# A dense last stage planned step by step: one list scheduler for every engine, and half of its output weights loaded early

## The chip, the cores and the metric

The kernel runs on one core of one Trainium2 chip. The core has five engines with a queue of instructions each: TensorE (PE, matrix products, with its weight loads shown as PEld), VectorE (DVE), ScalarE (ACT), GpSimd (POOL) and SyncE (SP), which issues most DMA transfers. An engine takes its instructions in the order in which they were written; it waits for the others through semaphores. The metric is the device time of one execution in microseconds (us). Before the change three runs took 922.58, 923.99 and 924.15 us.

## The reference

```python
# attention through 32 memory slots, 4 x 576 tokens (2304 in all), 8 heads of 64
a = softmax(phi, axis=sequence);  k_m, v_m = a.T @ k, a.T @ v
x = softmax(q @ k_m.T / 8) @ v_m                    # x: 2304 x 512
# mixture of experts: each token goes to 2 of 8 experts (512 -> 1024 -> 512)
out[token] = sum over its 2 experts of weight * (relu(x @ w1[e]) @ w2[e])
# dense last stage (512 -> 2048 -> 512)
h = out @ w_in
result = (h * cos(h)) @ w_out
```

All inputs are float32. The kernel carries each factor of a product as a high and a low float16 part and sums three products (high x high, low x high, high x low).

## The kernel before

The 2304 tokens are 18 tiles of 128. Attention and routing come first, then the eight experts (each over 5 tiles of gathered tokens), then the last stage. An expert's first layer (`l1`, tile `h`) is one group of 12 products per 128 of the 1024 columns, drained by ACT and DVE into `hT` (`l1_out`); its second (`l2`, tile `y`) makes 24 products per token tile, drained by ACT and written by DMA to a table `yd` in DRAM (`l2_out`).

The last stage goes by chunks of tiles: (0,2), (2,4), (4,8), (8,12), (12,16), (16,18). Here the chunks of two tiles are called narrow, those of four wide, and the first is chunk 0. What is done per tile `t` is `comb` (L962): POOL issues two gathers of rows of `yd` into `y0`, `y1`; ACT scales `y0` (L974); DVE adds the scaled `y1` (L975), finds the row's largest magnitude (L978), and makes a power-of-two scale and its inverses in six operations on one column each (L153 to L158, L981, L982); ACT and DVE split the row into a high and a low part `chl` (L984, L985); SP issues a transposing DMA into `x2T`. `c_bct` (L989) spreads the inverse scales of a chunk over all partitions by PE transposes `pb`, and ACT copies them to `bct`.

What is done per chunk and per 128 of the 2048 inner columns is called a unit here; each chunk has 16, f = 0 to 15. `m1` (L1027) makes 12 products `g` of 256 or 512 columns into one PSUM bank. Then come four DVE operations and two of ACT: `ty` (L1044, from PSUM), `tt` (L1045, rounding), `tt` (L1046, the remainder), ACT's sine (L1047), `ty` (L1048, from PSUM again, after which the bank is free), ACT's high part (L1049). POOL subtracts for the low part (L1050). `m2_` (L1052) multiplies both parts into output banks `o`, three products of 512 columns per tile, and after f = 15 ACT scales the bank out (L1066) and issues the store.

What sets the order: `at(t, fn)` records a call with a planned time and `issue` writes the calls in the order of these times. `chain(key, fn)` pins an operation behind the last one of the same key; what is not chained may be moved by the framework's own scheduler. In the last stage only the PE products are chained. PE's order is written out by a loop:

```python
    LAG = 3
...
        if u >= LAG:
            j, f = units[u - LAG]
            at(x, m2_, j, f)
```

so that `m2_` of a unit stands three units behind its `m1`. The times of `comb` and `c_bct` come from a formula on the start of the chunk before. `m1` takes its banks in turn from three (`ke` twice, `ha`), `m2_` from four. Row buffers: `l` (7 of 2 KB per partition) holds `y0`, `y1`, `chl` and the outputs; `s` (5 of 8 KB) holds raw expert weights earlier and `gT` in the last stage, four units to a buffer; `w` (4 of 16 KB) holds expert weights, then `win` and `wout`. Both halves of `wout` take such a `w` buffer, which comes free when the last expert's layers are done.

## Time and profile before

| | |
|---|---|
| time, median of 3 runs | 923.99 us |
| profiled execution, its own time | 923.57 us |
| its span in the trace | 921.8 us (1.77 us lie outside) |
| first product of the last stage | 532.54 us |
| first product of 512 columns there (chunk 2) | 619.91 us |
| last group of products begins | 910.03 us |
| PE busy, by engine record | 879.5 us (95%) |
| DVE / ACT / POOL busy | 583.5 / 467.7 / 215.0 us |

Products overlap on PE, and their ends are modelled, so "busy" says only that none was missing. How far apart two groups start is what PE really takes: 12 products of 256 columns about 1.31 us, six of 512 about 1.30 us. A wait shows as idle time before a row, with the engine and operation that ended it. For DVE, ACT and POOL a row's length is that of the operation and includes what it was held up after its start.

### The profile page before, as it was taken

How to read it: one execution, taken by the hardware profiler on the slowest of the kernel's cores; microseconds unless marked ns; L12 is line 12 of the kernel's file. 1: busy time of each engine (PE TensorE's matmuls, PEld its weight loads, DVE VectorE, ACT ScalarE, POOL GpSimd, SP SyncE). 2: the span in 40 equal slices, each digit the busy share in tenths (PEclk: the TensorE clock that was granted, in tenths of full speed). 3: DMA queues.
4: the chain of work that ended last, by engine and by line, in shares of the span. 5: the costliest groups of instructions: out<-in, count | busy, mean ns of one | idle time of the engine just before them, and what ended most of it. 6: DMA issues, size and time to landing. Idle time of an engine off the chain costs nothing.

```text
span 921.8 us, 14177 instructions
## 1 busy us (share of the span) xinstructions
PE 879.5 (95%) x5368; PEld 511.1 (55%) x5368; DVE 583.5 (63%) x1266; ACT 467.7 (51%) x830; POOL 215.0 (23%) x234
## 2 busy tenths in 40 slices
...
GB/s 352 395 298 90 116 159 254 268 278 240 235 256 252 289 236 282 231 307 266 206 197 113 171 160 67 95 46 69 80 1 13 155 17 12 68 12 1 1 46 23
DMA packets 108246, 146.55 MB, mean 159 GB/s; under 512 B 65808, under 2 KB 66448, under 8 KB 106128
## 3 DMA queue, kind: packets, MB, share of 16 engines
...
## 4 chain that ended last, share of the span: by engine, by line
PE 79%; DVE 7%; DMA 4%; issue 4%; ACT 3%; POOL 2%; SPq 0%; POOLq 0%; ACTq 0%; DVEq 0%
PE y L219 22%; PE h L219 21%; PE g L219 15%; PE o L219 15%; DMA y<-yd,sidx 2%; PE x L689 2%; PE kp L589 1%; DVE tt L1046 1%; PE sc L659 1%; DMA kvt<-in_kv 1%; DVE ty L1044 1%; ACT tt L1047 1%; DVE tt L1045 1%; POOL gT L1050 1%; POOL y L968 1%
## 5 line engine op out<-in xcount | busy, mean ns | idle before, releaser
L219 PE MATMUL h<-x,w 128*128 128x384 f16 (+1 forms) x1536 | 215.4, 302 | 9.7 <-DMA x<-xg 8.4
L219 PE MATMUL y<-w,hT 128*128 128x512 f16 x960 | 210.5, 379 | 0.0
L219 PE MATMUL g<-x2T,win 128*128 128x256 f16 (+1 forms) x1152 | 203.7, 327 | 4.5 <-DVE ty L1048 3.8
L219 PE MATMUL o<-wout,gT 128*128 128x512 f16 x864 | 202.6, 380 | 0.3 <-POOL gT L1050 0.2
L219 PEld LDWEIGHTS <-w 128*128 128x128 f16 x1536 | 151.6, 99 | 68.8 <-DMA x<-xg 8.5
L219 PEld LDWEIGHTS <-win 128*128 128x128 f16 x1152 | 113.2, 98 | 88.7 <-issue 5.7
L219 PEld LDWEIGHTS <-hT 128*128 128x128 f16 x960 | 93.9, 99 | 109.0
L1050 POOL TENSOR_TENSOR gT<-ty,gT 128x256 f16<-128x256 f32 (+1 forms) x96 | 93.0, 970 | 252.0 <-ACT gT L1049 249.8
L1047 ACT ACTIVATE tt<-tt,hp 128x256 f32<-128x256 f32 (+1 forms) x96 | 58.9, 614 | 163.2 <-DVE tt L1046 149.0
L219 PEld LDWEIGHTS <-gT 128*128 128x128 f16 x864 | 84.4, 98 | 93.9 <-POOL gT L1050 1.9
L219 DVE SCALAR_TENSOR_TENSOR w<-raw,wsc,w 128x1024 f16<-128x1024 f32 x64 | 81.1, 1287 | 32.8 <-ACT w L219 32.7
L219 DVE SCALAR_TENSOR_TENSOR hT<-h,hT 128x384 f16<-128x384 f32 (+1 forms) x128 | 61.5, 487 | 61.1 <-ACT hT L219 61.0
L1044 DVE SCALAR_TENSOR_TENSOR ty<-g,wis,bct 128x256 f32<-128x256 f32 (+1 forms) x96 | 58.8, 613 | 64.3 <-PE g L219 62.3
L1048 DVE SCALAR_TENSOR_TENSOR ty<-g,fac,tt 128x256 f32<-128x256 f32 (+1 forms) x96 | 59.1, 616 | 52.9 <-ACT tt L1047 52.4
L219 ACT ACTIVATE hT<-h 128x384 f16<-128x384 f32 (+1 forms) x128 | 55.3, 435 | 73.5 <-PE h L219 69.1
L1049 ACT ACTIVATE gT<-ty 128x256 f16<-128x256 f32 (+1 forms) x96 | 50.2, 523 | 64.5 <-DVE ty L1048 64.4
L829 POOL DMA_INDIRECT xg<-xd,idxB x24 | 26.0, 1085 | 216.0 <-DMA x<-xg 204.0
L219 ACT ACTIVATE w<-raw,wsc 128x1024 f16<-128x1024 f32 x64 | 71.7, 1140 | 5.0 <-ACT o L219 2.2
L1046 DVE SCALAR_TENSOR_TENSOR tt<-tt,ty 128x256 f32<-128x256 f32 (+1 forms) x96 | 68.5, 713 | 2.6
L219 ACT ACTIVATE junk<-raw 128x1024 bf16<-128x1024 f32 x64 | 67.3, 1052 | 3.8 <-ACT o L219 3.3
L219 ACT ACTIVATE o<-y,ysc 128x512 f32<-128x512 f32 x40 | 27.5, 686 | 68.2 <-PE y L219 68.2
L968 POOL DMA_INDIRECT y<-yd,sidx x36 | 36.1, 1002 | 87.4 <-DMA yd<-o 79.7
...
## 6 DMA issues: line engine op xcount, KB each, us to landing
...
yd<-o ACTq DMA_DIRECT2D x40, 256.0 KB, 6.7
...
xd<-hl SPq DMA_DIRECT2D x18, 256.0 KB, 2.4
```

The lines of the kernel that those rows point to most:

```text
L219: last[key] = fn(*a, **kw)
L589: T.matmul(kp[32 * j:32 * j + 32, g, :], lhsT=es[i][:, 32 * h:32 * h + 32], rhs=kvv[:, :, h * D:(h + 1) * D], start=(i == 0), stop=(i == 4))
L659: T.matmul(sc[p0:p0 + n, 64 * c:64 * c + 64], lhsT=qt[t // 8][:, c, c0:c0 + n], rhs=bdkt[b][:, c, :], start=True, stop=True)
L689: last[f"t{t}P"] = T.matmul(x[pn, g, 0:272], lhsT=eT[:, g, pn], rhs=bdv[b][:, g, :], start=True, stop=True)
L829: G.indirect_dma_start(out=g, out_offset=None, in_=xd[0:NA * P] if part == 0 else xd, in_offset=bass.IndirectOffsetOnAxis(ap=idx[:, col:co ...
L968: G.indirect_dma_start(out=y, out_offset=None, in_=yd[0:rows], in_offset=bass.IndirectOffsetOnAxis(ap=sidx[:, t, k:k + 1], axis=0))
L1044: V.scalar_tensor_tensor(y, ph[:, :n], wis[:, 2 * E + c:2 * E + c + 1], bct[j], op0=OP.mult, op1=OP.mult)
L1046: V.scalar_tensor_tensor(t, t, MAGIC, y, op0=OP.subtract, op1=OP.subtract)
L1047: A.activation(t, t, AF.Sin, bias=hp, scale=-2.0 * math.pi)
L1048: V.scalar_tensor_tensor(y, ph[:, :n], fac[:, c:c + 1], t, op0=OP.mult, op1=OP.mult)
L1049: A.activation(g[:, 0, :n], y, AF.Copy)
L1050: G.tensor_tensor(g[:, 1, :n], y, g[:, 0, :n], op=OP.subtract)
```

## The change

All of the last stage becomes one list of steps. `op` notes a step's engine, its assumed cost, what it calls and which steps it needs; `settle` places the whole list. Its inner `place` takes the steps by rank and puts each into the earliest free gap of its engine after its inputs; that is done forward, backward from the end and forward again, six times, and the best forward placement gives the planned times. Each step is now chained on its engine, the DMA issues of SP too, so the engines' order is the planner's and no longer the framework's.

With it: `comb` is cut into nine steps and the four operations between `m1` and `m2_` into seven; `LAG` is 4; `m1` of chunk 0 turns over five banks and that of the other chunks over three; `chl` takes buffers of the experts' gathered rows, and the outputs a buffer per chunk. The second half of `wout` goes, as two loads of 1 MB, into two of the five `s` buffers at a time within the last expert (`X[7]` is its start), which leaves three for `gT`; the first half stays in a `w` buffer and is issued 15.4 us before the planned start of the stage. The last two tiles' outputs leave by SP, and the last one is scaled half by ACT and half by DVE.

```diff
+    plan = []
+    LAT = dict(P=0.20, A=0.20, V=0.15, G=0.20, S=0.05, D=0.0)
+    ROUNDS = 6
+    def op(eng, cost, fn, *deps, lat=None):
+        flat = []
+        for d in deps:
+            flat += d if isinstance(d, (list, tuple)) else [d]
+        plan.append((eng, cost, fn, [d for d in flat if d is not None], LAT.get(eng, 0.0) if lat is None else lat))
+        return len(plan) - 1
+    def settle(goal, origin):
...
+        tail = [0.0] * n
+        for i in reversed(range(n)):
+            if i != goal:
+                tail[i] = max([tail[u] + lag(i, u) for u, _ in after[i]], default=-1000.0)
+        best = now = place([-x for x in tail], before)
+        for _ in range(ROUNDS):
+            end = place([-(t + c) for t, c in zip(now, cost)], after)
+            last_end = max(t + c for t, c in zip(end, cost))
+            now = place([last_end - t - c for t, c in zip(end, cost)], before)
+            if now[goal] < best[goal]:
+                best = now
+        for i in sorted(range(n), key=lambda i: (best[i], i)):
+            if plan[i][2]:
+                at(origin + best[i], plan[i][2])
+        return best
...
     def comb(t):
 
+        c = cm[t] = {}
...
+        def fetch(k):
+            c[k] = l2k([P, DM], F32, f"y{k}")
+            chain("G", G.indirect_dma_start, out=c[k], out_offset=None, in_=yd[0:rows],
+                  in_offset=bass.IndirectOffsetOnAxis(ap=sidx[:, t, k:k + 1], axis=0))
+        def first():
+            chain("A", A.activation, c[0], c[0], AF.Copy, scale=cw[:, t, 0:1])
+        def second():
+            chain("V", V.scalar_tensor_tensor, c[1], c[1], cw[:, t, 1:2], c[0], op0=OP.mult, op1=OP.add)
...
+        def high():
+            c["hl"] = xp.tile([P, 2 * DM], F16, tag="xg", name="chl", bufs=3).rearrange("p (w d) -> p w d", w=2)
+            chain("A", A.activation, c["hl"][:, 0], c[1], AF.Copy, scale=c["mx"][:, 1:2])
+        def low():
+            chain("V", V.scalar_tensor_tensor, c["hl"][:, 1], c[1], c["mx"][:, 1:2], c["hl"][:, 0], op0=OP.mult,
+                  op1=OP.subtract)
+        def turn():
+            if t == chunks[j][0]:
+                x2T[j] = mt([P, 8, (chunks[j][1] - t) * P], F16, "x2T")
+            chain("load", SP.dma_start_transpose, out=x2T[j][:, :, o], in_=c["hl"].rearrange("p w d -> p (w d)"))
+        return fetch, first, second, largest, scales, inverses, high, low, turn
...
     def load_wout(s):
-        wout.append(wp.tile([P, 4, 2, 2, DM], F16, tag="w", name="wout"))
-        SP.dma_start(wout[s].rearrange("p c w k f -> p c (w k f)"),
-                     wst[NCH + 4 * s:NCH + 4 * s + 4].rearrange("c p x -> p c x"))
+        n = (4, 2, 2)[s]
+        c0 = (0, 4, 6)[s]
+        w = hs("wout", 1, [P, n, 2, 2, DM], F16) if s else wp.tile([P, n, 2, 2, DM], F16, tag="w", name="wout")
+        wout.update((c0 + c, w[:, c]) for c in range(n))
+        chain("load", SP.dma_start, w.rearrange("p c w k f -> p c (w k f)"),
+              wst[NCH + c0:NCH + c0 + n].rearrange("c p x -> p c x"))
...
+    G_BANKS = (("ke", 1), ("ke", 1), ("ha", 0), ("yb", 0), ("hb", 0))
+    def bank_no(j, f):
+        return (16 * j + f) % 5 if j == 0 else (16 * j + f) % 3
+    def bank_of(j, f):
+        tag, early = G_BANKS[bank_no(j, f)]
+        return (ps if early else pools["ps"]).tile([P, 512], F32, tag=tag, name="g", bufs=2 if tag == "ke" else 1)
...
-        ph = bank_g()
+        ph = bank_of(j, f)
...
+    def wave(j, f):
...
+        def v1():
+            y = mt([P, 512], F32, "ty", 3)[:, :n]
+            ty[j, f] = y, mt([P, 512], F32, "tt", 3)[:, :n]
+            chain("V", V.scalar_tensor_tensor, y, ph(), wis[:, 2 * E + c:2 * E + c + 1], bct[j], op0=OP.mult, op1=OP.mult)
...
+        def sine():
+            y, t = ty[j, f]
+            chain("A", A.activation, t, t, AF.Sin, bias=hp, scale=-2.0 * math.pi)
...
+        def high():
+            if f % 4 == 0:
+                gT["all"] = hs("gT", 1, [P, 4, 2, 512], F16)
+            g = gT[j, f] = gT["all"][:, f % 4]
+            chain("A", A.activation, g[:, 0, :n], ty[j, f][0], AF.Copy)
+        def low():
+            g = gT[j, f]
+            chain("G", G.tensor_tensor, g[:, 1, :n], ty[j, f][0], g[:, 0, :n], op=OP.subtract)
+        return v1, v2, v3, sine, v4, high, low
...
+    def last_out(t):
+        j = ch_of[t]
+        if t == chunks[j][0]:
+            x2T[j, "o"] = hs("o", 0, [P, 4, DM], F32)
+        o = x2T[j, "o"][:, t - chunks[j][0]]
+        if t >= NT - 2:
+            half = DM // 2 if t == NT - 1 else DM
+            p = po.pop(t)
+            chain("A", A.activation, o[:, 0:half], p[:, 0:half], AF.Copy, scale=osc[:, t:t + 1])
+            if half < DM:
+                chain("V", V.tensor_scalar, o[:, half:], p[:, half:], osc[:, t:t + 1], None, op0=OP.mult)
+                chain("A", A.dma_start, out[t * P:(t + 1) * P, 0:half], o[:, 0:half])
+            chain("load", SP.dma_start, out[t * P:(t + 1) * P, DM - half:], o[:, DM - half:])
+            return
+        chain("A", A.activation, o, po.pop(t), AF.Copy, scale=osc[:, t:t + 1])
+        chain("A", A.dma_start, out[t * P:(t + 1) * P, :], o)
...
     m0 = x
-    LAG = 3
+    LAG = 4
+    back = 36.0
+    origin = m0 - back
+    rows_in = [ends[-11 - CA] + 3.0, ends[-10 - CA] + 3.0, ends[-3] + 4.5, ends[-2] + 4.5, ends[-1] + 8.0]
+    ready = [op(("ready", k), x - origin, None) for k, x in enumerate(rows_in)]
+    o_y, o_inv, turned, o_bct, m1s, m2s, v4s, lows, outs = {}, {}, {}, {}, {}, {}, {}, {}, {}
     units = [(j, f) for j in range(len(chunks)) for f in range(16)]
-    first = {}
+    o_m0 = op("m0_", back, None)
+    def put_comb(t):
+        fetch, first, second, largest, scales, inverses, high, low, turn = comb(t)
+        j = ch_of[t]
+        d = []
+        for k in range(2):
+            o = op("G", 1.25, lambda k=k: fetch(k), ready[min(t, 4)], o_y.get((t - 3 - (k == 0), 1 - k)),
+                   o_y.get("fetch"))
+            o_y["fetch"] = o
+            d.append(op("D", 1.05, None, o, lat=4.5))
+        a = op("A", 0.72, first, d[0])
+        o = op("V", 0.75, second, a, d[1])
+        o_y[t, 0] = o
+        o = op("V", 0.67, largest, o)
+        o = op("V", 0.36, scales, o)
+        o_inv[t] = op("V", 0.36, inverses, o)
+        o = op("A", 0.72, high, o, turned.get(t - 2))
+        o = o_y[t, 1] = op("V", 0.75, low, o)
+        o = op("S", 1.25, turn, o, [m1s[j - 2, 15]] if j > 1 else None)
+        turned[t] = op("D", 1.7, None, o, lat=2.5)
+    def put_bct(j, prev):
+        o = op("P", 0.1 * (chunks[j][1] - chunks[j][0]), lambda: c_bct(j), [o_inv[t] for t in range(*chunks[j])], prev)
+        o_bct[j] = op("A", 0.36 if len(range(*chunks[j])) == 2 else 0.55, lambda: c_bct_out(j), o,
+                      [v4s[j - 2, 15]] if j > 1 else None)
+        return o
+    def put_m1(j, f):
+        wide = chunks[j][1] - chunks[j][0] == 4
+        v1, v2, v3, sine, v4, high, low = wave(j, f)
+        u = units.index((j, f))
+        d = [turned[t] for t in range(*chunks[j])] if f == 0 else []
+        o = m = m1s[j, f] = op("P", 2.56 if wide else 1.30, lambda: m1(j, f), d, o_m0, prev,
+                                v4s.get(bank_no(j, f)))
+        o = op("V", 0.75 if wide else 0.46, v1, o, o_bct[j], lows.get(units[u - 3]) if u > 2 else None)
+        o = op("V", 0.48 if wide else 0.32, v2, o)
+        o = op("V", 0.80 if wide else 0.46, v3, o)
+        o = op("A", 0.75 if wide else 0.51, sine, o)
+        o = v4s[j, f] = v4s[bank_no(j, f)] = op("V", 0.75 if wide else 0.46, v4, o)
+        o = op("A", 0.62 if wide else 0.42, high, o, m2s.get(units[u - 17]) if u > 16 else None)
+        lows[j, f] = op("G", 1.2 if wide else 0.8, low, o)
+        return m
+    def put_m2(j, f):
+        o = prev
+        for t in range(*chunks[j]):
+            o = op("P", 0.645, lambda t=t: m2_(j, f, t), lows[j, f], o,
+                   outs.get(t - 4) if f == 0 else None)
+            if f == 15:
+                outs[t] = op("A", 1.05, lambda t=t: last_out(t), o)
+        m2s[j, f] = o
+        return o
+    for j in range(2):
+        for t in range(*chunks[j]):
+            put_comb(t)
+    prev = put_bct(0, op("bct", back - 6.0, None))
     for u in range(len(units) + LAG):
         if u < len(units):
             j, f = units[u]
-            if f == 0:
-                first[j] = x
-            at(x, m1, j, f)
-            x += 1.31 if chunks[j][1] - chunks[j][0] == 2 else 2.59
+            prev = put_m1(j, f)
+            if f == 13 and j + 1 < len(chunks):
+                prev = put_bct(j + 1, prev)
         if u >= LAG:
-            j, f = units[u - LAG]
-            at(x, m2_, j, f)
-            x += 0.65 * (chunks[j][1] - chunks[j][0])
-    y = [ends[-11 - CA + t] + 3.0 for t in range(2)] + [m0 + 3.0, m0 + 6.0]
-    for j in range(2, len(chunks)):
-        a, b = chunks[j]
-        y += [first[j - 1] + (first[j] - first[j - 1] - 20.0) / (b - a) * k for k in range(b - a)]
-    for t in range(NT):
-        j = ch_of[t]
-        at(y[t], comb, t)
-        if t == chunks[j][1] - 1:
-            at(first[j] - 5.3, c_bct, j)
+            prev = put_m2(*units[u - LAG])
+        if u < len(units) and f == 15 and j + 2 < len(chunks):
+            for t in range(*chunks[j + 2]):
+                put_comb(t)
+    start_of = settle(prev, origin)
...
-    at(X[7] + 45.0, load_wout, 0)
-    at(m0 + 4.0, load_wout, 1)
+    at(X[7] + 17.2, load_wout, 1)
+    at(X[7] + 17.3, load_wout, 2)
+    at(m0 - 15.4, load_wout, 0)
```

The order of DVE's instructions shows what the planner made of it. In the kernel after, `chain` stands in L286 for all of them.

First place: DVE's queue as the last expert's second part of `l1` begins (hT are its drains; y, cmx, cmt, ib, osc and chl belong to `comb` of tile 0). Before:

```order
L975 SCALAR_TENSOR_TENSOR y_5426<-y_5426,cw,y_5425 128x512
L978 TENSOR_REDUCE cmx<-y_5426 128x1
L153 TENSOR_SCALAR cmt<-cmx 128x1
L154 TENSOR_SCALAR cmt<-cmt 128x1
L155 TENSOR_SCALAR cmx<-cmt 128x1
L158 TENSOR_SCALAR ib<-cmx 128x1
L981 TENSOR_SCALAR cmx<-ib 128x1
L982 TENSOR_TENSOR osc<-ib,ik 128x1
L985 SCALAR_TENSOR_TENSOR chl<-y_5426,cmx,chl 128x512
L219 SCALAR_TENSOR_TENSOR hT<-h,hT 128x384 x5
L975 SCALAR_TENSOR_TENSOR y_5479<-y_5479,cw,y_5478 128x512
```

After the change:

```order
L286 SCALAR_TENSOR_TENSOR hT<-h,hT 128x384 x3
L286 SCALAR_TENSOR_TENSOR y_5431<-y_5431,cw,y_5429 128x512
L286 TENSOR_REDUCE cmx<-y_5431 128x1
L286 TENSOR_SCALAR cmt<-cmx 128x1
L286 TENSOR_SCALAR cmt<-cmt 128x1
L286 TENSOR_SCALAR cmx<-cmt 128x1
L286 SCALAR_TENSOR_TENSOR hT<-h,hT 128x384
L286 TENSOR_SCALAR ib<-cmx 128x1
L286 TENSOR_SCALAR cmx<-ib 128x1
L286 TENSOR_TENSOR osc<-ib,ik 128x1
L286 SCALAR_TENSOR_TENSOR chl<-y_5431,cmx,chl 128x512
L286 SCALAR_TENSOR_TENSOR hT<-h,hT 128x384
```

Three of the drains `hT` now stand ahead of tile 0's sum `y`, and a fourth ahead of its inverses.

Second place: DVE's queue in chunk 0 (a unit is `ty` from g and wis, `tt`, `tt`, `ty` from g and fac; y is the sum of a tile of a later chunk). Before, at the sum of tile 4:

```order
L1048 SCALAR_TENSOR_TENSOR ty<-g,fac,tt 128x256
L1044 SCALAR_TENSOR_TENSOR ty<-g,wis,bct 128x256
L1045 TENSOR_SCALAR tt<-ty 128x256
L1046 SCALAR_TENSOR_TENSOR tt<-tt,ty 128x256
L975 SCALAR_TENSOR_TENSOR y_6187<-y_6187,cw,y_6186 128x512
L1048 SCALAR_TENSOR_TENSOR ty<-g,fac,tt 128x256
L1044 SCALAR_TENSOR_TENSOR ty<-g,wis,bct 128x256
L978 TENSOR_REDUCE cmx<-y_6187 128x1
L1045 TENSOR_SCALAR tt<-ty 128x256
L153 TENSOR_SCALAR cmt<-cmx 128x1
```

After the change, at the sums of tiles 2 and 3:

```order
L286 SCALAR_TENSOR_TENSOR ty<-g,wis,bct 128x256
L286 SCALAR_TENSOR_TENSOR ty<-g,fac,tt 128x256
L286 TENSOR_SCALAR tt<-ty 128x256
L286 SCALAR_TENSOR_TENSOR tt<-tt,ty 128x256
L286 SCALAR_TENSOR_TENSOR y_5684<-y_5684,cw,y_5652 128x512
L286 SCALAR_TENSOR_TENSOR ty<-g,fac,tt 128x256
L286 SCALAR_TENSOR_TENSOR ty<-g,wis,bct 128x256
L286 TENSOR_SCALAR tt<-ty 128x256
L286 SCALAR_TENSOR_TENSOR tt<-tt,ty 128x256
L286 SCALAR_TENSOR_TENSOR y_5704<-y_5704,cw,y_5686 128x512
L286 SCALAR_TENSOR_TENSOR ty<-g,fac,tt 128x256
L286 SCALAR_TENSOR_TENSOR ty<-g,wis,bct 128x256
```

The sums of `comb` stand between a unit's remainder (`tt` from tt and ty) and the `ty` that waits for ACT's sine; those here belong to the next chunk, and that of tile 4 now comes four units later.

Third place: DVE's queue late in the chunk before the first wide one, where the last parts `chl` are made. Before (the `chl` of tile 7, in chunk 1 too):

```order
L1044 SCALAR_TENSOR_TENSOR ty<-g,wis,bct 128x256
L158 TENSOR_SCALAR ib<-cmx 128x1
L1048 SCALAR_TENSOR_TENSOR ty<-g,fac,tt 128x256
L1045 TENSOR_SCALAR tt<-ty 128x256
L981 TENSOR_SCALAR cmx<-ib 128x1
L982 TENSOR_TENSOR osc<-ib,ik 128x1
L985 SCALAR_TENSOR_TENSOR chl<-y_6422,cmx,chl 128x512
L1046 SCALAR_TENSOR_TENSOR tt<-tt,ty 128x256
L1044 SCALAR_TENSOR_TENSOR ty<-g,wis,bct 128x256
```

After the change (unit f = 11 of chunk 1, the `chl` of tiles 6 and 7):

```order
L286 TENSOR_SCALAR ib<-cmx 128x1
L286 TENSOR_SCALAR cmx<-ib 128x1
L286 TENSOR_TENSOR osc<-ib,ik 128x1
L286 SCALAR_TENSOR_TENSOR tt<-tt,ty 128x256
L286 SCALAR_TENSOR_TENSOR chl<-y_6085,cmx,chl 128x512
L286 SCALAR_TENSOR_TENSOR chl<-y_6169,cmx,chl 128x512
L286 SCALAR_TENSOR_TENSOR ty<-g,fac,tt 128x256
L286 SCALAR_TENSOR_TENSOR ty<-g,wis,bct 128x256
L286 TENSOR_SCALAR tt<-ty 128x256
L286 SCALAR_TENSOR_TENSOR tt<-tt,ty 128x256
L286 SCALAR_TENSOR_TENSOR ty<-g,wis,bct 128x256
```

Before, one `chl` stands in a unit; now a unit holds several tiles' inverses and two `chl` on end, in front of the `ty` that frees its bank.

## Rows read from the trace of the kernel before

**Rows 1.** The page's first line.
```profile
span 921.8 us, 14177 instructions
```

**Rows 2.** Waits of PE, 490 to 922: waiter, releaser, total us, times, longest.
```profile
PE g L219 <- DVE ty L1048: 3.8, 3, 2.1
PE h L219 <- DVE hT L219: 1.0, 1, 1.0
```

**Rows 3.** Timeline of PE: start, us, operation, count, [idle before, releaser].
```profile
500.02 7.96 PE L219 MATMUL h<-x,w 128*128 128x384 f16 x48
508.98 7.96 PE L219 MATMUL h<-x,w 128*128 128x384 f16 x48 [1.00 <-DVE hT L219]
...
532.54 5.55 PE L219 MATMUL g<-x2T,win 128*128 128x256 f16 x48
...
540.53 1.46 PE L219 MATMUL o<-wout,gT 128*128 128x512 f16 x6
541.82 1.47 PE L219 MATMUL g<-x2T,win 128*128 128x256 f16 x12
543.13 1.46 PE L219 MATMUL o<-wout,gT 128*128 128x512 f16 x6
...
562.63 2.63 PE L219 MATMUL g<-x2T,win 128*128 128x256 f16 x12 [2.07 <-DVE ty L1048]
...
619.91 2.75 PE L219 MATMUL g<-x2T,win 128*128 128x512 f16 x12
...
910.03 5.71 PE L219 MATMUL o<-wout,gT 128*128 128x512 f16 x24
```

**Rows 4.** Three windows: busy us (count) by engine, PE clock, DMA share, GB/s.
```profile
532.50:619.90 87.40, 82.78 (x565) 55.79 (x564) 71.12 (x185) 38.01 (x79) 34.40 (x41) 0.98 0.36 93
560.00:570.00 10.00, 7.93 (x44) 4.89 (x43) 8.13 (x22) 3.37 (x7) 4.50 (x5) 0.83 0.27 67
619.90:910.00 290.10, 290.10 (x1445) 141.46 (x1444) 188.72 (x339) 101.13 (x165) 87.64 (x83) 1.00 0.15 39
```

**Rows 5.** Timeline of DVE, same columns.
```profile
504.06 0.75 DVE L975 SCALAR_TENSOR_TENSOR y<-y,cw,y 128x512 f32<-128x512 f32 x1 [13.02 <-DMA y<-yd,sidx]
...
557.67 0.42 DVE L1046 SCALAR_TENSOR_TENSOR tt<-tt,ty 128x256 f32<-128x256 f32 x1
561.43 0.75 DVE L975 SCALAR_TENSOR_TENSOR y<-y,cw,y 128x512 f32<-128x512 f32 x1 [3.33 <-DMA y<-yd,sidx]
...
579.04 0.48 DVE L1048 SCALAR_TENSOR_TENSOR ty<-g,fac,tt 128x256 f32<-128x256 f32 x1 [0.64 <-ACT tt L1047]
579.44 0.47 DVE L1044 SCALAR_TENSOR_TENSOR ty<-g,wis,bct 128x256 f32<-128x256 f32 x1
579.95 0.29 DVE L1045 TENSOR_SCALAR tt<-ty 128x256 f32<-128x256 f32 x1
580.28 0.78 DVE L1046 SCALAR_TENSOR_TENSOR tt<-tt,ty 128x256 f32<-128x256 f32 x1
```

**Rows 6.** Timeline of POOL beside the last DVE row above.
```profile
580.05 0.72 POOL L1050 TENSOR_TENSOR gT<-ty,gT 128x256 f16<-128x256 f32 x1 [1.93 <-ACT gT L1049]
```

**Rows 7.** Groups of DVE by shape, 525 to 922: count, busy us, mean ns, idle.
```profile
L985 DVE SCALAR_TENSOR_TENSOR chl<-y,cmx,chl 128x512 f16<-128x512 f32 x16 | 12.7, 793 | 0.0
...
L978 DVE TENSOR_REDUCE cmx<-y 128x1 f32<-128x512 f32 x16 | 10.9, 679 | 0.2
...
L155 DVE TENSOR_SCALAR cmx<-cmt 128x1 int32<-128x1 int32 x16 | 2.4, 151 | 0.3
```

**Rows 8.** DMA issues, 480 to 922: count, KB each, median us to landing.
```profile
wout<-wst SPq DMA_DIRECT2D x2, 2048.0 KB, 9.1
...
yd<-o ACTq DMA_DIRECT2D x6, 256.0 KB, 7.0
...
x2T<-chl SPq DMA_TRANSPOSE x18, 3.1
```

**Rows 9.** Timeline of ACT at the end.
```profile
915.13 1.33 ACT L1066 ACTIVATE o<-o,osc 128x512 f32<-128x512 f32 x2 [1.23 <-PE o L219]
```

More of the change, by code (lines that the diff above doesn't have):

```diff
@@ L1 @@
+import bisect
+import heapq
 import math
@@ L994, in c_bct, with c_bct_out @@
             _, o = c_place(t)
-            chain("P", T.transpose, pb[:, o], cm.pop(t)[:, 2:3].to_broadcast([P, P]), ident)
+            chain("P", T.transpose, pb[:, o], cm.pop(t)["mx"][:, 2:3].to_broadcast([P, P]), ident)
+        bct[j] = pb
+    def c_bct_out(j):
+        a, b = chunks[j]
+        pb = bct[j]
         bct[j] = mt([P, 512], F32, "bct")[:, :(b - a) * P]
-        A.activation(bct[j], pb[:, :(b - a) * P], AF.Copy)
-    win, wout = [], []
+        chain("A", A.activation, bct[j], pb[:, :(b - a) * P], AF.Copy)
+    win, wout = [], {}
     def load_win(s):
@@ L1046, in m1 @@
[L1046 to L1067 removed]
+        pg[j, f] = ph
```

116 lines of the change are left out of this document (68 added, 48 removed).

## Prediction

> **What bounds the kernel now.** I read the page's first line (a span of 921.8 us [rows 1]), then PE's waits in the last stage, PE's timeline, three windows, and DVE's timeline where PE waited. PE is the bound: in the wide stretch from 619.9 to 910.0 it shows 290.10 us busy of 290.10 at a granted clock of 1.00 [rows 4], so nothing the change does there can gain. Losses can only lie before, in the narrow chunks 0 and 1, and at the end.
>
> From the first `g` at 532.54 to the first of 512 columns at 619.91 PE takes 87.37 us [rows 3]. Its work there is 32 groups `m1` at 1.31 (541.82 to 543.13), 29 tile pairs of `m2_` at 1.29 (540.53 to 541.82) and two broadcasts `pb` of six transposes, which I estimate at 0.6 from a product's 0.11 (1.31 over 12): 41.9 + 37.4 + 0.6 = 79.9. So 7.4 us are lost. Of these 3.8 are three waits for the `ty` that frees a bank [rows 2]; the longest, 2.07 before 562.63, is followed by twelve products in 2.63 where 1.47 is normal [rows 3], in a window whose clock is 0.83 [rows 4]: part of it ran at 1.2 instead of 2.4 GHz after PE had stood still. The rest are shorter stops of the same kind. The cause of the longest stands on DVE: at 557.67 it does a `tt`, then waits 3.33 us for the gathered rows of `comb`'s sum `y` until 561.43 [rows 5]; behind that sum, in order, stands the `ty` for which PE waits. In undisturbed units (579.04 to 580.28) DVE itself stands 0.64 waiting for the sine.
>
> Two smaller losses: 1.00 us before 508.98, where PE waits for `hT` [rows 3], because DVE stood 13.02 us for the first gathered tile [rows 5]; and at the end 24 products take 5.71 where four times 1.29, and 0.17 of overhang (1.46 less 1.29), make 5.33: 0.4. In all 7.4 + 1.0 + 0.4 = 8.8 us can be had from PE.
>
> **Part by part.** *Drains before the sum of tile 0* (first place of the order). The fourth to eighth groups of `h` no longer queue behind the gather: 1.0 is gained if the data come by the time the third drain is done (about 506.5: 500.02 + 3 x 1.99, with 1.99 a quarter of 7.96, and the drain), which 504.06 satisfies.
>
> *Early half of `wout`.* Two loads of 1 MB stand on SP's queue ahead of the transposes of tiles 0 and 1. The trace has no such load; the nearest row is 2 MB in 9.1 us [rows 8]. From one side they cost nothing: they are done long before the ninth unit of chunk 0 needs them. From the other they hold up the first gather by 9.1. Then tile 0's sum is ready near 513, ACT's first scaling stands in front of the third drain, and PE waits about 1.8 for a bank instead of 1.0: the term lies between -1.0 and +0.8, and I take -1.0, since gathers and loads ran beside each other in the trace. The first half of `wout` waits for its buffer as before.
>
> *The planned order in the narrow chunks* (second place). Gathers are now issued several units before their sums, so the waits of 3.33 and 13.02 go. A sum stands in DVE's 0.64 us of waiting for the sine. What is late next is DVE itself. A unit with such a piece costs it 0.40 + 0.51 + 0.33 (starts 579.04, 579.44, 579.95, 580.28) + 0.78 + about 0.64 for the piece (sum 0.75 [rows 5], `chl` 0.79, maximum 0.68 [rows 7], each overlapping the next start by about 0.1): 2.66. PE's unit is 1.31 + 1.29 = 2.60. So DVE falls back 0.06 per unit; a unit with two tiles' three small operations (0.15 each [rows 7], 0.19 with their dependence) adds 6 x 0.19 - 0.64 = 0.5; the unit in the third place adds twelve of them and two `chl`, 2.2 + 1.4 - 0.64 = 3.0, but some four units without a piece run on end and win back 0.85 each. Followed through chunk 1 this makes DVE about 4.2 late at f = 11. PE needs that bank three units later: 3 x 2.60 less the 1.29 of an `m2_`, less the 2.2 from `m1` to the freeing `ty` (0.3 + 0.51 + 0.33 + 0.42 + 0.64), plus `pb` 0.4: 4.7. It fits by half a microsecond, and the `pb` of chunk 2, which needs the inverses made just before, by as little. I therefore take 6.4 of the 7.4, leaving 1.0; the bounds are all of it, and 3 to 4 kept where ACT's extra copies (0.7) put the sine off in a few units.
>
> *Five banks in chunk 0 and LAG 4.* Five banks remove the bank wait there; between `m1` of a unit and its `m2_` there are now four units, 10.4 us less the 2.6 of one, against about 4 from a product's end to its `gT`. At the end five units of `m2_` follow the last `m1` instead of four, and the 0.4 goes. `gT` with three buffers holds 12 units and needs at most nine: nothing. The wide chunks hide the rest: DVE is busy 188.72 and POOL 87.64 of 290.10 there [rows 4], with units twice as long, so batches of three gathers that now stand in front of a `gT` on POOL stay under PE's products; were that cover gone, each would show as up to four units' slack lost, which no row there comes near.
>
> *End.* Two scalings take 1.33 on ACT at 915.13 [rows 9]; with the last one halved between ACT and DVE 0.3 goes, from 0.2 to 0.4 for the copies, and the DMA of half the bytes gives between nothing and 0.6. I take 0.3.
>
> Sum: 1.0 + 6.4 + 0.4 + 0.3 = 8.1. The profiled execution took 923.57 (0.42 under the median 923.99): 923.57 - 8.1 = 915.5; with 0.3 for the median lying higher, 915.8.
>
> **Where a rule of the skill speaks against it.** The `tt` before the sine takes 0.42 alone (557.67) and 0.78 where POOL's `gT` runs beside it (580.05 to 580.77) [rows 5, 6]. The Trainium skill, SBUF — State Buffer, "Who interferes with whom", says that a DVE instruction with two SBUF inputs contends with a GpSimd instruction that reads SBUF, and that whoever comes second blocks fully. The sums and `chl` have two such inputs, too; by that rule, the trace agreeing for `tt`, a piece put beside a `gT` may be held as well.
>
> **Rivals.** *Partial.* The order does what it says, but DVE's lateness passes the 4.7 in chunk 1 by 3 to 5 us: gain 3 to 5, 918.5 to 921. For it speaks the margin of 0.5 and DVE's 71.12 busy of 87.40 now [rows 4], which must fit into 80; against it that four units of slack return the lateness when no piece is due.
>
> *No change.* The planner's assumed arrival is too early at the start of the stage: ACT's first scaling of tile 2 now stands before the first sine, and POOL's gathers of tile 3 before the first `gT`. They wait for the store of the last expert's fourth tile, 7.0 to land [rows 8]: its products end near 526 (531.5 less four times 1.29), it has landed by 534, two gathers make 536.5, and PE wants the first `gT` at 538.5 (531.5 + 5 x 1.31 + two of its products). Were the landing 10 later, the gain would be gone: 923.
>
> *Slower.* DVE and POOL hold each other up. If in each of the 32 narrow units the piece is held by what `tt` is held now (0.78 - 0.42 = 0.36), DVE loses 11.5 more; with the 4.2 late, less 4.7 of slack, PE waits about 11: 8.8 of gains turn into 2.2 of loss, 925.8. It decides from 10.7 of new waiting, 0.33 per unit. Against it: a `gT` lasts 0.72, once in 2.6 us, and mostly meets only one operation.
>
> **How the numbers follow.** Full gain (914 to 918) 0.61; partial (918 to 922) 0.20; no change 0.09; slower 0.10. About 0.2% (1.85 us) is what a measurement here can tell from nothing: faster by more (below 922.1) 0.81, within 0.09, slower 0.10. The low end is every term at its bound: 923.57 - 8.8 - 1.0 = 913.8. The high end takes in the partial rival up to 921.5, which leaves 0.2 above.
>
> **What would show it.** PE without idle before the fifth group of `h`, and the first `g` near 531.5; the first product of 512 columns 79 to 80 us after it; no DVE row before a sum that waits for a gather; `g` rows late in chunk 1 with at most a microsecond of idle; the last group of `o` with no wait for `gT`. I am wrong if `g` or `pb` around f = 11 to 14 of chunk 1 waits several microseconds, if the first product of 512 columns waits for a transpose (3.1 to land [rows 8], the last `chl` some 5 us ahead), or if DVE's `tt`, sums and `chl` are longer than now.

## The result and the profile after

The changed kernel takes 913.1 us (median of 4 runs, 912.79 to 913.58) against 924.07 (922.58 to 925.82) in the same comparison: ratio 0.9881, interval 0.9863 to 0.9899, 11.0 us faster. The forecast was 915.8, and the measured time lies 0.7 below the range's low end. The direction and the place of the gain were right; sizes were off, and these four runs came out about 1 us below six later ones of the same kernel, whose median of 914.22 lies inside the range.

The page of the profiled execution (912.87) begins with the line that answers to [rows 1], then the busy time of each engine, then PE's two costliest lines of the stage (count, busy us, mean ns, idle before).

```profile
span 911.1 us, 14175 instructions
...
PE 874.9 (96%) x5368; PEld 509.5 (56%) x5368; DVE 586.4 (64%) x1267; ACT 468.8 (51%) x830; POOL 213.5 (23%) x234
...
L286 PE MATMUL g<-x2T,win 128*128 128x256 f16 (+1 forms) x1152 | 202.2, 326 | 0.0
L286 PE MATMUL o<-wout,gT 128*128 128x512 f16 x864 | 201.5, 379 | 0.0
```

The idle of `g` and `o` is 0.0; the waits of [rows 2] have no successor. The timeline of PE, as in [rows 3], with one group of `h` ahead of all that was changed:

```profile
486.17 2.78 PE L286 MATMUL h<-x,w 128*128 128x256 f16 x24
...
498.93 15.76 PE L286 MATMUL h<-x,w 128*128 128x384 f16 x96
...
530.29 6.71 PE L286 MATMUL g<-x2T,win 128*128 128x256 f16 x60
...
602.18 0.60 PE L286 MATMUL pb<-ident,cmx 128*128 128x128 f32 x4
602.62 1.46 PE L286 MATMUL o<-wout,gT 128*128 128x512 f16 x6
603.92 1.47 PE L286 MATMUL g<-x2T,win 128*128 128x256 f16 x12
...
609.13 2.75 PE L286 MATMUL g<-x2T,win 128*128 128x512 f16 x12
...
899.24 6.64 PE L286 MATMUL o<-wout,gT 128*128 128x512 f16 x30
```

The groups of `h` run through without the stop at the fifth, `pb` of chunk 2 and the first `g` of 512 columns follow without idle, and the last 30 products of `o` take 6.64, five times 1.29 and the overhang. From the first `g` to the first of 512 columns it is 78.84 us instead of 87.37.

DVE's groups in that stretch, as in [rows 7] (the same view of before has 5.5 us of idle ahead of the sums `y`, 4.3 of them for gathers, and 7.8 ahead of the freeing `ty`):

```profile
L286 DVE SCALAR_TENSOR_TENSOR tt<-tt,ty 128x256 f32<-128x256 f32 x31 | 19.0, 614 | 0.8
L286 DVE SCALAR_TENSOR_TENSOR ty<-g,fac,tt 128x256 f32<-128x256 f32 x31 | 14.8, 478 | 0.5 <-ACT tt L286 0.2
L286 DVE SCALAR_TENSOR_TENSOR y<-y,cw,y 128x512 f32<-128x512 f32 x8 | 6.3, 792 | 0.0
```

No sum waits for a gather, and DVE's wait for the sine has shrunk to 0.2. Where it is latest, in chunk 1 up to f = 11, DVE's timeline shows:

```profile
589.54 0.48 DVE L286 SCALAR_TENSOR_TENSOR ty<-g,fac,tt 128x256 f32<-128x256 f32 x1
...
592.19 0.48 DVE L286 SCALAR_TENSOR_TENSOR ty<-g,fac,tt 128x256 f32<-128x256 f32 x1
...
594.87 0.48 DVE L286 SCALAR_TENSOR_TENSOR ty<-g,fac,tt 128x256 f32<-128x256 f32 x1
...
598.79 0.14 DVE L286 TENSOR_SCALAR ib<-cmx 128x1 int32<-128x1 int32 x1
...
600.27 0.15 DVE L286 TENSOR_TENSOR osc<-ib,ik 128x1 f32<-128x1 f32 x1
600.34 0.42 DVE L286 SCALAR_TENSOR_TENSOR tt<-tt,ty 128x256 f32<-128x256 f32 x1
600.68 1.41 DVE L286 SCALAR_TENSOR_TENSOR chl<-y,cmx,chl 128x512 f16<-128x512 f32 x2
602.00 0.48 DVE L286 SCALAR_TENSOR_TENSOR ty<-g,fac,tt 128x256 f32<-128x256 f32 x1
```

Units with a piece follow each other in 2.65 and 2.68 (589.54, 592.19, 594.87), the 2.66 of the working; twelve operations on one column take 1.6 (598.79 to 600.42), where 2.2 were assumed, and the `tt` of that unit (600.34) takes 0.42, where 0.78 was assumed. The freeing `ty` of f = 11 is done at 602.48; PE wants its bank at 603.92. The margin is 1.4, not 0.5.

The sum of tile 0, ahead of which DVE stood 13.02 [rows 5], stands right behind the third drain now:

```profile
506.11 0.72 ACT L286 ACTIVATE y<-y,cw 128x512 f32<-128x512 f32 x1 [2.58 <-DMA y<-yd,sidx]
...
507.24 0.56 DVE L286 SCALAR_TENSOR_TENSOR hT<-h,hT 128x384 f16<-128x384 f32 x1 [3.13 <-ACT hT L286]
507.71 0.74 DVE L286 SCALAR_TENSOR_TENSOR y<-y,cw,y 128x512 f32<-128x512 f32 x1
```

ACT still waits 2.58 for the gathered rows ahead of its part of that drain; PE runs on.

The end of the program, answering to [rows 9]: ACT, DVE and the queues (SPq, ACTq: a DMA is issued):

```profile
905.30 1.09 ACT L286 ACTIVATE o<-o,osc 128x512 f32<-128x512 f32 x2 [0.42 <-PE o L286]
906.02 1.26 SPq L286 DMA_DIRECT2D out<-o  x2
906.42 0.34 ACTq L286 DMA_DIRECT2D out<-o  x1
906.42 0.48 DVE L286 TENSOR_SCALAR o<-o,osc 128x256 f32<-128x256 f32 x1 [3.67 <-ACT o L286]
```

Half of the last tile still leaves on ACT's queue; SP sends the other half and the tile before. DVE's half starts not with PE's last product (899.24 + 6.64 = 905.88) but when ACT's half is done.

### The profile page after: what moved, and what is told of

Same layout as the page of the kernel before. It is cut to its first block, busy times and chain, and to the rows that moved or that the text cites. A ratio compares the mean times of both kernels' runs of the same rounds, so it can differ in the third digit from the quotient of the medians.

```text
span 911.1 us, 14175 instructions
## 1 busy us (share of the span) xinstructions
PE 874.9 (96%) x5368; PEld 509.5 (56%) x5368; DVE 586.4 (64%) x1267; ACT 468.8 (51%) x830; POOL 213.5 (23%) x234
## 4 chain that ended last, share of the span: by engine, by line
PE 86%; DVE 4%; issue 4%; ACT 2%; DMA 2%; POOL 1%; ACTq 0%; SPq 0%; POOLq 0%; DVEq 0%
PE h L286 22%; PE y L286 22%; PE g L286 19%; PE o L286 18%; PE x L756 1%; DVE tt L286 1%; PE kp L656 1%; PE sc L726 1%; DMA kvt<-in_kv 1%; DVE ty L286 1%; ACT tt L286 1%; POOL xg L896 1%; DMA xg<-xd,idxB 0%; ACT o L286 0%; PE sums L286 0%
## 5 line engine op out<-in xcount | busy, mean ns | idle before, releaser
L286 PE MATMUL h<-x,w 128*128 128x384 f16 (+1 forms) x1536 | 215.1, 301 | 9.1 <-DMA x<-xg 8.7
L286 PE MATMUL y<-w,hT 128*128 128x512 f16 x960 | 210.5, 379 | 0.0
L286 PE MATMUL g<-x2T,win 128*128 128x256 f16 (+1 forms) x1152 | 202.2, 326 | 0.0
L286 PE MATMUL o<-wout,gT 128*128 128x512 f16 x864 | 201.5, 379 | 0.0
L286 PEld LDWEIGHTS <-w 128*128 128x128 f16 x1536 | 151.5, 99 | 68.0 <-DMA x<-xg 8.8
L286 PEld LDWEIGHTS <-win 128*128 128x128 f16 x1152 | 112.7, 98 | 83.9
L286 PEld LDWEIGHTS <-hT 128*128 128x128 f16 x960 | 93.9, 99 | 109.0
L286 POOL TENSOR_TENSOR gT<-ty,gT 128x256 f16<-128x256 f32 (+1 forms) x96 | 90.9, 947 | 246.2 <-ACT gT L286 246.0
L286 ACT ACTIVATE tt<-tt,hp 128x256 f32<-128x256 f32 (+1 forms) x96 | 59.0, 614 | 156.0 <-DVE tt L286 149.7
L286 PEld LDWEIGHTS <-gT 128*128 128x128 f16 x864 | 84.6, 98 | 91.8
L286 DVE SCALAR_TENSOR_TENSOR hT<-h,hT 128x384 f16<-128x384 f32 (+1 forms) x128 | 61.6, 486 | 77.4 <-ACT hT L286 77.2
L286 DVE SCALAR_TENSOR_TENSOR w<-raw,wsc,w 128x1024 f16<-128x1024 f32 x64 | 81.0, 1286 | 32.8 <-ACT w L286 32.7
L286 DVE SCALAR_TENSOR_TENSOR ty<-g,wis,bct 128x256 f32<-128x256 f32 (+1 forms) x96 | 58.8, 612 | 66.3 <-PE g L286 64.2
L286 ACT ACTIVATE hT<-h 128x384 f16<-128x384 f32 (+1 forms) x128 | 55.5, 435 | 75.9 <-PE h L286 72.5
L286 DVE SCALAR_TENSOR_TENSOR ty<-g,fac,tt 128x256 f32<-128x256 f32 (+1 forms) x96 | 59.0, 615 | 45.0 <-ACT tt L286 44.3
L286 ACT ACTIVATE gT<-ty 128x256 f16<-128x256 f32 (+1 forms) x96 | 50.2, 523 | 62.2 <-DVE ty L286 60.9
L286 ACT ACTIVATE w<-raw,wsc 128x1024 f16<-128x1024 f32 x64 | 71.7, 1140 | 4.7 <-ACT o L286 2.1
L286 DVE SCALAR_TENSOR_TENSOR tt<-tt,ty 128x256 f32<-128x256 f32 (+1 forms) x96 | 69.6, 725 | 3.0
L286 ACT ACTIVATE junk<-raw 128x1024 bf16<-128x1024 f32 x64 | 67.3, 1052 | 3.9 <-ACT o L286 3.4
L286 ACT ACTIVATE o<-y,ysc 128x512 f32<-128x512 f32 x40 | 27.5, 687 | 67.3 <-PE y L286 66.2
L286 POOL DMA_INDIRECT y<-yd,sidx x36 | 35.2, 979 | 86.5 <-DMA yd<-o 79.3
```

What stands on the lines that cost most here:

```text
L286: last[key] = fn(*a, **kw)
```

## The experiments

One table from all traces shows most of it. "Mark" is the start of the group of 24 products of `h` that stands at 486.17 above; no step ahead of it was changed in the source. The other columns are stretches in us; where PE takes five units of `m2_` after the last `m1` instead of four, one of 1.30 moves from the narrow column into the wide one.

| kernel | mark | to first `g` | narrow: to first 512-column `g` | wide: to PE's last product | to the end |
|---|---|---|---|---|---|
| before | 487.25 | 45.29 | 87.37 | 295.83 | 6.1 |
| before, again | 487.71 | 45.29 | 87.40 | 295.81 | 6.1 |
| before, tile 0 later | 485.31 | 44.13 | 86.91 | 295.83 | 6.0 |
| changed | 486.17 | 44.12 | 78.84 | 296.75 | 5.2 |
| changed, again | 488.07 | 44.13 | 78.83 | 296.76 | 5.2 |
| no lead planned | 485.44 | 51.78 | 85.92 | 296.76 | 5.2 |
| gathers late | 487.12 | 44.39 | 92.66 | 304.7 | 5.2 |
| LAG 3 | 487.02 | 44.46 | 80.13 | 295.96 | 6.0 |
| three banks | 487.49 | 44.12 | 80.71 | 296.75 | 5.2 |
| `wout` as before | 485.32 | 44.13 | 78.83 | 296.76 | 5.2 |
| old end | 485.77 | 44.12 | 78.84 | 296.75 | 5.2 |
| two engines | 487.09 | 44.12 | 78.84 | 296.75 | 5.2 |
| maximum twice | 488.13 | 44.12 | 80.07 | 296.75 | 5.2 |
| maximum three times | 485.87 | 44.12 | 83.23 | 296.75 | 5.2 |

**Both kernels again.** No edit.

> The kernel before, unchanged, traced once more. In its first trace the first product of h starts at 106.37 us and a group of 24 products of h at 487.42; in the trace of the changed kernel the same stand at 105.14 and 486.17, 1.25 earlier, though no instruction before 487 was changed on purpose. Theory 1: this offset is a spread between executions (arrival of the first loads); then this trace lies anywhere between 105.1 and 106.5 and 486.1 and 487.6, and the 1.25 is no gain of the change. Theory 2: it belongs to the program (other places of tiles in SBUF, another queue order); then 106.3 to 106.5 and 487.3 to 487.5 again. The time: 924.0, within 0.1%.

> The changed kernel unchanged, traced and timed once more. In the ten traces so far the group of 24 products of h, which stands ahead of every changed instruction, starts anywhere from 485.31 to 487.71 us, in kernels with the change and without it. Theory 1: that spread belongs to the execution; then this trace may lie anywhere in it, the stretch behind the mark is again 44.12 to the first g, 78.84 to the first of 512 columns and 296.75 to PE's last product, and a median of more runs lies 1 us above or below 913.1 (the sum of the stage's own gains, 9.4, from the 923.6 of before gives 914.1). Theory 2: the change draws the first part 1.1 us ahead; then the mark is at 485.8 to 486.3 and the median at 912.8 to 913.4.

Measured: before 923.58 (12 runs, 921.9 to 925.85), changed 914.22 (6 runs, 912.62 to 914.79; ratio 0.9896, 0.9878 to 0.9914). PE's timeline of the changed kernel again:

```profile
107.27 5.30 PE L286 MATMUL h<-x,w 128*128 128x256 f16 x24 [8.73 <-DMA x<-xg]
...
488.07 2.78 PE L286 MATMUL h<-x,w 128*128 128x256 f16 x24
...
532.20 6.71 PE L286 MATMUL g<-x2T,win 128*128 128x256 f16 x60
...
611.03 2.75 PE L286 MATMUL g<-x2T,win 128*128 128x512 f16 x12
...
901.15 6.64 PE L286 MATMUL o<-wout,gT 128*128 128x512 f16 x30
```

The first `h` starts at 107.27; in the first trace of the same kernel it was

```profile
105.14 5.30 PE L286 MATMUL h<-x,w 128*128 128x256 f16 x24 [8.70 <-DMA x<-xg]
```

and yet every stretch behind the mark agrees to 0.01. Over fourteen traces the mark spreads from 485.31 to 488.13, and the first `h` from 105.02 to 107.36, with and without the change: the spread belongs to the execution and arises mostly before 107 us. The 487.42 in the first text is the place of that group in the view of the chain that ended last; in the timeline it starts at 487.25, so the offset to the changed kernel is 1.08 and not 1.25. The second trace of before ruled out neither theory (its 106.84 and 487.71 lie outside both windows); the changed kernel's two traces, 1.9 apart, settle it. It is not a difference between chips alone: 23 runs of before on one chip range from 920.97 to 925.07. Of the 10.7 us between the first two traces 1.1 is this spread. All ten runs of the changed kernel have a median of 913.5, 57 runs of before in all comparisons 923.4: the change gains 9.9, and the stage itself 9.6.

**Tile 0 behind the drains, alone.** In the kernel before:

```diff
-    y = [ends[-11 - CA + t] + 3.0 for t in range(2)] + ...
+    y = [ends[-11 - CA + 1] + 2.9, ends[-11 - CA + 1] + 3.0] + ...
```

> The kernel before with the whole step of tile 0 (gathers, sum, maximum, transpose) moved to just before the step of tile 1, so that the third drain of h no longer queues behind its gather. Theory 1: the wait of PE for hT, 1.00 us in the trace of before, was the whole cost of the old place: 923.0, no wait for hT, the first g about 1.0 earlier against the group of h at 487.42, the narrow chunks as before (87.4). Theory 2: the stop before the fifth drain only moves to a later one, because the gathers of tile 0 now end in the middle of the drains: PE waits for hT at another place, 0.5 to 3 us, and the time is 924 to 926.

921.86 (12 runs) against 922.93; ratio 0.9989, 0.9980 to 0.9999.

```profile
485.31 2.78 PE L219 MATMUL h<-x,w 128*128 128x256 f16 x24
...
529.44 5.55 PE L219 MATMUL g<-x2T,win 128*128 128x256 f16 x48
```

The stretch to the first `g` is 44.13 instead of 45.29: the whole first term, 1.16, from this edit alone, and nothing was lost later (the narrow chunks were 0.46 shorter, too).

**The lead of the gathers.** First the planner is told that rows arrive at once:

```diff
-            d.append(op("D", 1.05, None, o, lat=4.5))
+            d.append(op("D", 0.0, None, o, lat=0.0))
```

> The changed kernel with the planner told that a gather's rows are there as soon as it is issued (0 instead of 4.5 + 1.05 us); all else of the list is the same, so sums are still put where DVE has a gap, but right behind their gathers. Theory 1: what gains is the distance between a gather and its sum; then DVE stands about 3 us before the sums of tiles 2 to 5 and the drains of tile 0 and 1's place are held again, PE waits for g and hT, and 5 to 8 of the 8.2 us gained in the narrow part are lost: 918 to 921. Theory 2: what gains is one small piece per unit in DVE's waits for the sine, and four units of slack carry a single wait of 3 us: 913 to 915.

927.83 against 922.93, ratio 1.0060 (1.0046 to 1.0073): slower than before. PE's waits in the stage:

```profile
PE g L286 <- DVE ty L286: 5.6, 5, 1.8
PE h L286 <- DVE ib L286: 3.7, 1, 3.7
PE h L286 <- DVE hT L286: 1.8, 2, 1.1
```

The drains lose 7.7 and the narrow chunks 7.1, together more than theory 1 allowed. Since the sums moved too, a second kernel keeps DVE's order and moves only the gathers of tiles 2 and up to the place of ACT's scaling:

```diff
-            o = op("G", 1.25, lambda k=k: fetch(k), ...
+            o = op("G", 1.25, (lambda k=k: fetch(k)) if t < 2 else None, ...
-        a = op("A", 0.72, first, d[0])
+        a = op("A", 0.72, first if t < 2 else lambda: (fetch(0), fetch(1), first()), d[0])
```

> The changed kernel with the order of DVE and PE as it is, but from tile 2 on both gathers of a tile stand on POOL's queue right before the step in which ACT scales their rows (about one unit of 2.6 us ahead of the sum), not four units ahead. Theory 1: the distance between gather and sum is what the narrow chunks gained; then DVE stands again 2 to 4 us before the sums of tiles 3 to 7, PE waits for ty, and 4 to 7 of the 7.2 gained from the first g to the first of 512 columns are lost: 83 to 86 us there, 917 to 920. Theory 2: the places of the sums (later, one small piece per unit) gained it; then the four units of slack take the waits, 79 to 80.5 us, 913 to 915.

933.6 against 923.85, ratio 1.0101 (1.0081 to 1.0121). Theory 2 fails, and theory 1's size was wrong: 13.8 lost in the narrow chunks and 8.0 in the wide ones. In the two traces DVE and ACT do the same operations in the same order. ACT's, DVE's and PE's timelines where it is worst:

```profile
568.81 0.72 ACT L286 ACTIVATE y<-y,cw 128x512 f32<-128x512 f32 x1 [6.77 <-DMA y<-yd,sidx]
...
569.75 0.49 ACT L286 ACTIVATE tt<-tt,hp 128x256 f32<-128x256 f32 x1
```

```profile
570.27 0.48 DVE L286 SCALAR_TENSOR_TENSOR ty<-g,fac,tt 128x256 f32<-128x256 f32 x1 [5.50 <-ACT tt L286]
```

```profile
569.89 2.74 PE L286 MATMUL o<-wout,gT 128*128 128x512 f16 x6 [5.21 <-ACT gT L286]
```

ACT stands 6.77 at the head of its queue for the gathered rows; the sine behind it holds DVE 5.50, and `gT` holds PE 5.21. I had counted the wait on DVE alone; on ACT a gather that is late stops the sine and `gT`, where the four units of slack lie. After that stop six products take 2.74 instead of 1.46: from 569 to 573 the granted clock is 0.50, that is 1.2 GHz, and that is part of the loss. With the same order of DVE, the whole gain in the narrow chunks, and more, is thus lost without the lead. That shows that the lead is needed, not that it is enough: the order of before with only its gathers moved ahead, or only chained, was not run, so the share of the sums' new places stays open.

**DVE's margin.** The maximum of tiles 4 to 7 is taken two or three times:

```diff
+            for _ in range(2 if 4 <= t < 8 else 1):
                 chain("V", V.tensor_reduce, c["mx"][:, 0:1], c[1], ...
```

> The changed kernel with the maximum of tiles 4 to 7 taken twice (the same result), unknown to the planner: 0.67 us more on DVE for each of four tiles. In the trace DVE's freeing ty of f = 11 ends at 602.48 and its bank is wanted at 603.92, 1.4 later; the inverses end at 600.4 and pb stands at 602.18. Theory 1 (DVE's lateness against that margin): units with a piece take 2.66 of PE's 2.60, so nothing is won back, 2.0 to 2.7 are added, and PE waits 0.6 to 1.3 us near the end of chunk 1: 79.4 to 80.1 from the first g to the first of 512 columns. Theory 2: DVE's waits for the sine take it: 78.84. Theory 3: no slack at all: 81.5.

> As the kernel with the maximum taken twice, but three times: 5.4 us more on DVE in all. Theory 1: 2.6 to 4.0 us of waiting at the end of chunk 1, in places of g and pb: 81.4 to 82.8 from the first g to the first of 512 columns, with the clock lower for a moment if one wait passes 2 us, as in the kernel before. Theory 2: 78.84 to 79.2. Theory 3: 84.2.

914.56 and 917.37 against 923.66 (4 runs each). The narrow stretch grows by 1.23 and 4.39 us. PE's one stop in the first:

```profile
606.86 1.47 PE L286 MATMUL g<-x2T,win 128*128 128x256 f16 x12 [0.50 <-DVE ty L286]
```

Added were 4 x 0.67 = 2.7 and 5.4; less the margin of 1.4 that makes 1.3 and 4.0. So theory 1 holds: lateness within the margin was free, and what went beyond it was paid about in full; the second came 0.4 dearer, above theory 1's 82.8. No single wait was longer than 1.23, and the granted clock stayed at 1.00.

**Five banks, LAG 4, the early weights.** Each undone alone:

```diff
-        return (16 * j + f) % 5 if j == 0 else (16 * j + f) % 3
+        return (16 * j + f) % 3
```

> The changed kernel with three banks for g in chunk 0, as before, planned anew. Theory 1: at the start of the stage four or five m1 (1.31 us each) run with no m2_ between them; with three banks the fourth needs the freeing ty of the first, which comes some 4.1 us after its start against 3.9, and the fifth that of the second, 6.1 against 5.2: PE waits about 1 us there, 914.1, 79.9 from the first g to the first of 512 columns. Theory 2: the five banks are never needed: 913.1, 78.8.

915.99 against 923.85. The wait is where theory 1 puts it, with nearly twice the price, 1.87:

```profile
537.41 2.78 PE L286 MATMUL g<-x2T,win 128*128 128x256 f16 x24 [1.71 <-DVE ty L286]
```

LAG = 3:

> The changed kernel with LAG 3, planned anew. Theory 1 (terms of the prediction): the last group of o is again 24 products with a wait of 0.2 to 0.4, and between a unit's m1 and its m2_ there is one unit (2.6 us) less, which DVE's lateness of about 3.3 in chunk 1 just uses up: 0.4 to 1.5 lost, 913.5 to 914.6. Theory 2: only the tail's 0.4 counts: 913.5. The time from the last landing of out to the end of the span is 3.2 us before and 2.3 after; if LAG sets it, it is 3.2 again here and 0.9 more are lost; if not, 2.3.

915.62 against 923.85, a microsecond above theory 1. In the narrow chunks nothing is lost (80.13 is 78.84 and one `m2_`), but 0.3 are lost before the first `g`. The last 24 products of `o` take 5.84, 0.5 more than four units and the overhang, and to the end it is 6.0, 0.8 more: the scalings of two earlier tiles, which the order puts off to the end, now hold ACT when the last product comes. From the last issue of `out` to the end of the span it is 4.2 in both traces, so the lag does not set that time. In all LAG 4 is worth about 1.6 here.

The output weights in two loads of 2 MB, the second after the stage has begun, as before:

> The changed kernel with the output weights loaded as before: two loads of 2 MB into the buffers of the input weights, the second one after the stage has begun. Theory 1 (the prediction): the early loads neither cost nor gain: 913.1, 78.8 from the first g to the first of 512 columns, no wait of PE for wout. Theory 2: the late second half is what the transposes of tiles 2 and 3 then stand behind on SP's queue, or what the ninth unit waits for: 1 to 3 lost, 914 to 916. Theory 3: the early loads hold up the gathers of tiles 0 and 1 (issued 3.7 later than before in the two traces); without them the time falls below 912.8.

912.38 against 923.85 (changed kernel: 0.9881, this: 0.9879, 0.9860 to 0.9899). All stretches are the same; the early loads neither gain nor cost PE. They do hold up the first gather: it is issued 16.7 us after the mark with them (502.86) and 12.0 without (497.28), and ACT's wait of 2.58 above is gone without them; the drains' slack covers it. The time lies where theory 3 put it, but no stretch is shorter, so it is theory 1 that holds.

**The end.** With the end of before (each tile scaled whole by ACT, sent on ACT's queue):

> The changed kernel with the end of before: every output tile is scaled whole by ACT into a row buffer of its own and sent on ACT's queue. Theory 1, the two traces: from PE's last product to the end of the span 6.06 us before and 5.22 after, so this loses 0.84: 913.9, 5.9 to 6.2 in its trace. Theory 2, the prediction's term: only the shorter scaling counts, 0.3: 913.4, 5.5 in its trace. Nothing else in the stage moves: 78.8 from the first g to the first of 512 columns in both.

912.59 against 922.93, and 5.2 to the end as with the split: both theories fail. ACT at the end:

```profile
905.70 0.34 ACTq L286 DMA_DIRECT2D out<-o  x1
906.14 0.69 ACT L286 ACTIVATE o<-o,osc 128x512 f32<-128x512 f32 x1 [0.47 <-ACT o L286]
906.85 0.34 ACTq L286 DMA_DIRECT2D out<-o  x1
```

ACT waits 0.47 for the issue of its own DMA ahead of the second scaling, since the new order chains them; the last issue comes 1.37 after PE's last product, with the split 1.05, before the change 0.8. So the split wins back about half of what the chaining costs, and the end does not follow: 5.2 with either. Issues and landings of `out` in the second trace of before, and in the changed kernel:

```profile
L1067 ACTq DMA_DIRECT2D out<-o x2: 338/338/339, 916.3 to 917.0; - x2
...
DMA to landing us min/median/max: 2.1/2.1/2.1
```

```profile
L286 SPq DMA_DIRECT2D out<-o x2: 344/347/350, 906.0 to 906.9; - x2
...
DMA to landing us min/median/max: 1.9/2.0/2.1
```

The last rows land at 917.0 + 2.1 = 919.1 and at 906.9 + 1.9 = 908.8, 2.9 after PE's last product in both. Then the span goes on for 3.2 us with the end of before (two traces show the landing), 2.2 to 2.3 with the split end and 1.8 with the old end in the new order (906.85 + 2.0 to 910.7). That stretch, in which no engine shows work, is where the 0.8 went; what sets it stays open.

Another end: DVE scales the last tile but one and ACT the last, so that each engine reads a bank of its own:

> The changed kernel with another end: of the last two tiles DVE scales the first whole and ACT the second whole, each sent on its own queue, where now ACT scales one and a half and DVE's half starts only when ACT's half is done (906.42, 0.54 after PE's last product). Theory 1: DVE then waits for ACT because both read one bank, and with a bank each the last issue comes 0.72 us after PE's last product instead of 1.05: 0.3 gained in the trace of the end, 4.9 instead of 5.2, 912.8. Theory 2: the end of the span does not follow the last issue (with the old end under the new plan it was 5.22 too, though its last issue was 0.3 later): 5.2 again.

913.89 against 914.22 for the changed kernel in the same comparison.

```profile
906.19 0.75 DVE L286 TENSOR_SCALAR o<-o,osc 128x512 f32<-128x512 f32 x1 [2.49 <-PE o L286]
...
907.56 0.34 ACTq L286 DMA_DIRECT2D out<-o  x1
```

DVE now starts when its tile's last product is done, and the last issue comes 0.76 after PE's last product instead of 1.05, but with 256 KB instead of 128; the end stays at 5.2, as theory 2 has it. No version beats the changed kernel by more than these measurements can tell.

## Why the prediction was right in kind and wrong in size

The forecast lay 2.7 too high (915.8 against 913.1). Of this 1.5 is the sum of the terms (8.1 forecast, 9.6 measured), 0.3 is what was added for the median, and the remaining 0.9 is spread between executions, which no term contained. With the terms as measured the time is 914.0, just inside the range; what put it outside is the spread.

- *PE is the bound; losses lie in front of the wide stretch and at the end.* Right: wide is 295.83 and 296.75 less one `m2_` of 1.30, and the difference of 0.38 is the tail.
- *Drains before the sum, 1.0.* Right: 1.17, 1.16 by itself. The two early loads held up the first gather by about 4.7, not 9.1, and the drains' slack covered it.
- *The planned order: "I therefore take 6.4 of the 7.4, leaving 1.0".* This step failed. Less the one `m2_` that moved out, 87.37 - 78.84 - 1.30 = 7.23 were won, and no idle of `g` or `o` is left. Mechanism and unit price were right (2.66). But the last unit of the lateness was priced too high (twelve operations 1.6, not 2.2; its `tt` 0.42, not 0.78), so the margin was 1.4, and lateness inside a margin costs nothing, so there was no reason to hold back 1.0 for it.
- *LAG 4 and the tail, 0.4.* Right for the tail: 0.38. With LAG 3 the new order loses about 1.6, and with three banks 1.87, which the sum held inside the order's term.
- *End, 0.3.* This step failed, too, in size and reason: 0.84, though the last rows land no sooner after PE's last product (2.9 in both); it lies in the stretch behind the last landing, and its cause stays open. No run shows the bound of 0.6 for a DMA of half the bytes, on which the low end rests in part: 128 and 256 KB all land in 1.9 to 2.1.
- *The base.* This step put the time outside the range. "The low end is every term at its bound: 923.57 - 8.8 - 1.0" takes the executions' common part as fixed, and 0.3 was added because the median of three lay higher. The part before 107 us alone spreads by 2.3 us, and over 57 runs the median is 0.2 lower than 923.57. The terms measured are 1.17 + 7.23 + 0.38 + 0.84 = 9.6. On which side of the low end (913.8) a few runs fall is chance: the first four have a median of 913.1, the six later ones 914.22, all ten 913.5.
- *Rivals.* Partial: the lateness never passed the margin. No change: the gathers of tiles 2 and 3 came in time. Slower: `tt` lasts 614 ns on average in the narrow stretch and the sums 792, against 575 and 747 before: 31 x 0.04 and 8 x 0.045, some 1.6 us of DVE's time, where by the prediction 10.7 of new waiting were needed for a slower kernel. One sum of the eight was held, the one that began just after a `gT` of POOL:

```profile
543.74 0.67 POOL L286 TENSOR_TENSOR gT<-ty,gT 128x256 f16<-128x256 f32 x1 [1.09 <-ACT gT L286]
```

```profile
543.79 1.17 DVE L286 SCALAR_TENSOR_TENSOR y<-y,cw,y 128x512 f32<-128x512 f32 x1
```

The other seven took 0.74: where a `gT` fell into such a unit, it ran beside the `tt` and was over when the sum began, or began after the sum. The rule of the Trainium skill (SBUF — State Buffer, "Who interferes with whom") thus held for `tt` and for the sums; the sums seldom met its condition.
